# Loading the MLP weights during the convolution, and computing mish in groups of eight and six chunks instead of four

## The chip, the core and the metric

The kernel runs on one NeuronCore of a Trainium2 chip. The core has a matrix engine (TensorE, PE in the profile), a vector engine (VectorE, DVE), an engine for activation functions (ScalarE, ACT), a general engine (GpSimd, POOL) and a queue engine that starts transfers (SyncE, SP). Each runs its own list of instructions in order, and they wait for one another only through semaphores. Data lies in SBUF (128 partitions) and, for the results of matmuls, in PSUM. The metric is the time of one execution on the device in microseconds (us); "span" is the time from the first to the last instruction in the profiled execution.

## What is computed

One block of a network with 2048 tokens of 640 features. `A_ref` is a long convolution whose kernel is made from the parameters; `B_ref` is an MLP with the activation mish, h·tanh(log(1+exp(h))), and a hidden width of 1728.

```python
def _B_ref(x, w1, b1, w2):
    h = jnp.einsum("bsd,df->bsf", x, w1) + b1
    sp = jnp.log1p(jnp.exp(-jnp.abs(h))) + jnp.where(h > 0, h, jnp.zeros_like(h))
    act = h * jnp.tanh(sp)
    return jnp.einsum("bsf,fd->bsd", act, w2)

x = A_u
h = x + _A_ref(_layernorm(x, axis=-1), ...)      # convolution over the tokens, cut here
h2 = h + _B_ref(_layernorm(h, axis=-1), B_w1, B_b1, B_w2)
return h2
```

## The kernel before

The kernel is a sequence of stages. First come the tables and the convolution's kernel (parameters `AreT` ... `DskB`, scratch `rr`, `tth`, `Prr`, `Pii`, `Hr_t`, `Hin_t`, ...), then the forward transform and the products with the planes `PKc`, `PKs`, `qv` (results in `Yr_t`, `Ysn_t`), then the inverse transform, the residual sum in `xs`, the second layer norm and its transposition into `ln2T`, and last the MLP. SBUF is handed out by stacks of contexts: what is entered in `esA2` is given back when the kernel of the convolution is done, `esB` holds the transform's buffers, and `esC`, opened when `esB` and `esA` have been closed, holds everything of the MLP, its weights included. So the weights lie where buffers of the transform lay, and their load waits until these are no longer read:

```python
esC = ExitStack()
esC.__enter__()
EC = esC.enter_context
w1s = EC(nc.sbuf_tensor([P, ND, F], BF16))
w2s = EC(nc.sbuf_tensor([P, NFT, D], BF16))
b1s = EC(nc.sbuf_tensor([P, NFT], FP32))
mishT = EC(nc.sbuf_tensor([P, NFT, 2, 512], BF16))
NPD1 = 3
pd1 = EC(nc.psum_tensor([P, NPD1, FF], FP32))
po = EC(nc.psum_tensor([P, 2, 1024], FP32))
# ... (views of the weights in DRAM)
@block.gpsimd
def _(gp):
    gp.wait_ge(s_vyf.sem, h_done_v)          # the last residual sum
    gp.wait_ge(s_pei.sem, 2 * NFR)           # the last matmul of the inverse transform
    gp.wait_ge(s_ped.sem, 2 * NFR)
    gp.wait_ge(s_aed.sem, 4 * 2 * NFR)
    gp.dma_start(w1s[:], w1_v).then_inc(s_x.sem, 16)
    gp.dma_start(w2s[:, 0:13, :], w2_v).then_inc(s_x.sem, 16)
    # ... the last 64 rows of w2, and b1 in two pieces
w_loaded = s_x.n
```

The MLP works on four blocks of 512 tokens (`sc`). A block has 14 chunks of the hidden width (`ft`; 13 of 128 rows and one of 64). A chunk is five matmuls on PE (`dense1_chunk`, into one of three PSUM buffers), the addition of the bias by DVE into a slot of `ebuf` (`dve_h_evac`), then Exp, Ln(1+x) and Tanh on ACT, a chunk or a pair of chunks at a time, and the product h·tanh on DVE into `mishT` (`dve_mish_mult`). When all 14 products of a block are there, PE computes its four token tiles of the second product (`dense2_stile`, 28 matmuls each), and DVE adds them to `xs` (`dve_out_tile`). ACT works by groups of chunks; PE and DVE follow the same groups:

```python
NSLOT = 8
ebuf = EC(nc.sbuf_tensor([P, NSLOT, 3, FF], BF16))
GROUPS = [[0, 1, 2, 3], [4, 5, 6, 7], [8, 9, 10, 11], [12, 13]]

def dense1_chunk(pe, sc, ft):
    ci = sc * NFT + ft
    if ci >= NPD1:
        pe.wait_ge(s_vm.sem, ci - NPD1 + 1)      # PSUM buffer free: chunk ci-3 evacuated
    # ... five matmuls

def dense2_stile(pe, st):
    if st >= 2:
        pe.wait_ge(s_vo.sem, st - 1)             # PSUM buffer free: tile st-2 added
    sc = st // 4
    pe.wait_ge(s_vm2.sem, (sc + 1) * NFT)        # all 14 products of the block
    # ... 14 matmuls of 512 columns, 14 of 128

@block.tensor
def _(pe):
    pe.wait_ge(s_x.sem, w_loaded)
    for sc in range(SC):
        pe.wait_ge(s_aet.sem, min(NT, 4 * sc + 4))
        for gi, grp in enumerate(GROUPS):
            for ft in grp:
                dense1_chunk(pe, sc, ft)
            if sc >= 1:
                dense2_stile(pe, (sc - 1) * 4 + gi)
    for st in range(12, 16):
        dense2_stile(pe, st)

def act_group(ac, sc, grp):
    ac.wait_ge(s_vm.sem, base + grp[-1] + 1)     # the whole group is in ebuf
    # ... ops: pairs of chunks where two slots lie side by side, else single chunks
    for rows, h_ap, sp_ap, th_ap, n in ops:
        s_am.tick(ac.activation(sp_ap, h_ap, ACT.Exp))
    ac.wait_ge(s_am.sem, s_am.n)
    for rows, h_ap, sp_ap, th_ap, n in ops:
        s_am.tick(ac.activation(sp_ap, sp_ap, ACT.Ln, bias=cst[0:rows, 1:2]))
    ac.wait_ge(s_am.sem, s_am.n)
    for rows, h_ap, sp_ap, th_ap, n in ops:
        last = s_am.tick(ac.activation(th_ap, sp_ap, ACT.Tanh))

def dve_mish_mult(vc, sc, ft):
    vc.wait_ge(s_am.sem, act_done_val[(sc, ft)]) # the last Tanh of the chunk's group
    # ... h * tanh

@block.vector
def _(vc):
    for sc in range(SC):
        for gi, grp in enumerate(GROUPS):
            for ft in grp:
                dve_h_evac(vc, sc, ft)
            if gi >= 1:
                for ft2 in GROUPS[gi - 1]:
                    dve_mish_mult(vc, sc, ft2)
            if sc >= 1:
                dve_out_tile(vc, (sc - 1) * 4 + gi)
        for ft2 in GROUPS[-1]:
            dve_mish_mult(vc, sc, ft2)
    for st in range(12, 16):
        dve_out_tile(vc, st)
```

`dve_h_evac` of chunk number ci (counted over all blocks) also waits until the slot's previous owner, ci-NSLOT, has been multiplied.

Of the kernel before, what the change touches and what calls it, by code (L numbers as in the profile page):

```python
# [9 lines left out]
FP32 = mybir.dt.float32  # L10
BF16 = mybir.dt.bfloat16
# [19 lines left out]
def bass_sequential_preLN__ssm_conv_s4__dense_activation_mish__prompt_kernel(  # L31
# [4 lines left out]
    L = 2048  # L36
    D = 640
    F = 1728
    P = 128
    NT = L // P  # L40
    ND = D // P
    FF = 512
    HB = 256
    NFR = L // HB
    NB = 32
    NA = 8
    NFT = 14
    FLAST = F - 13 * P
# [9 lines left out]
    s_x = mkev("s_x")  # L58
    s_parT = mkev("s_parT")
    s_wk = mkev("s_wk")  # L60
# [8 lines left out]
    s_ak = mkev("s_ak")  # L69
    s_pe = mkev("s_pe")  # L70
    s_vev = mkev("s_vev")
    s_pef = mkev("s_pef")
    s_vpl = mkev("s_vpl")
    s_ped = mkev("s_ped")
    s_aed = mkev("s_aed")
    s_vyf = mkev("s_vyf")
    s_pei = mkev("s_pei")
# [14 lines left out]
    EP = esP.enter_context  # L92
# [10 lines left out]
    l2st = EP(nc.sbuf_tensor([P, NT, 2, 6], FP32))  # L103
    l2mv = EP(nc.sbuf_tensor([P, NT, 2], FP32))
    l2rs = EP(nc.sbuf_tensor([P, NT, 2], FP32))
    ln2T = EP(nc.sbuf_tensor([P, ND, L], BF16))
    ln2t = EP(nc.sbuf_tensor([P, 2, D], BF16))
    ident = EP(nc.sbuf_tensor([P, P], BF16))
    identf = EP(nc.sbuf_tensor([P, P], FP32))
# [2 lines left out]
    block = EP(nc.Block())  # L112

    x_tok = A_u.rearrange("b (t p) d -> p t (b d)", p=P)

    esA = ExitStack()
    esA.__enter__()
    EA = esA.enter_context
    PKc = EA(nc.sbuf_tensor([P, 2, D], BF16))
    PKs = EA(nc.sbuf_tensor([P, 2, D], BF16))  # L120
    qv = EA(nc.sbuf_tensor([P, D], BF16))
    AreT = EA(nc.sbuf_tensor([P, D], BF16))
    AimT = EA(nc.sbuf_tensor([P, D], BF16))
    BreT = EA(nc.sbuf_tensor([P, D], BF16))
    BimT = EA(nc.sbuf_tensor([P, D], BF16))
    CreT = EA(nc.sbuf_tensor([P, D], BF16))
    CimT = EA(nc.sbuf_tensor([P, D], BF16))
    ldtB = EA(nc.sbuf_tensor([P, D], BF16))
    DskB = EA(nc.sbuf_tensor([P, D], BF16))
    dtB = EA(nc.sbuf_tensor([P, D], FP32))  # L130
    rr = EA(nc.sbuf_tensor([P, D], FP32))
    tth = EA(nc.sbuf_tensor([P, D], FP32))
    Prr = EA(nc.sbuf_tensor([P, D], FP32))
    Pii = EA(nc.sbuf_tensor([P, D], FP32))
    lnst = EA(nc.sbuf_tensor([P, NT, 2, 6], FP32))
    lnmv = EA(nc.sbuf_tensor([P, NT, 2], FP32))
    lnrs = EA(nc.sbuf_tensor([P, NT, 2], FP32))

    esA2 = ExitStack()
    esA2.__enter__()  # L140
    EA2 = esA2.enter_context
    tmp4 = EA2(nc.sbuf_tensor([P, 4, HH], FP32))
    Hr_t = EA2(nc.sbuf_tensor([P, NB, HH], BF16))
    Hin_t = EA2(nc.sbuf_tensor([P, NB, HH], BF16))
# [12 lines left out]
    @block.gpsimd  # L157
    def _(gp):
        gp.dma_start(xs[:], x_tok).then_inc(s_x.sem, 16)
        s_x.n += 16  # L160
        s_pln.tick(gp.memset(mhalf[:], -0.5))
        s_pc.tick(gp.memset(identf[:], 0.0))
        gp.wait_ge(s_pc.sem, s_pc.n)
        s_pc.tick(gp.affine_select(out=identf[:], in_=identf[:], compare_op=ALU.not_equal, fill=1.0, base=0,
                                   pattern=[[-1, P]], channel_multiplier=1))
        s_pc.tick(gp.iota(qi[:, 0, 0:HB], [[1, HB]], base=0, channel_multiplier=0))
        s_pc.tick(gp.iota(qi[:, 0, HB:FF], [[1, HB]], base=0, channel_multiplier=0))
        gp.wait_ge(s_pc.sem, s_pc.n)
        s_pc.tick(gp.iota(qi[:, 0, HB:HB + 1], [[1, 1]], base=256, channel_multiplier=0))
        s_pc.tick(gp.iota(mci[:, 0:1], [[0, 1]], base=0, channel_multiplier=1))  # L170
        s_pc.tick(gp.iota(qi[:, 1, 0:HB], [[1, HB]], base=256, channel_multiplier=0))
# [117 lines left out]
    wk_loaded = s_wk.n  # L289
# [203 lines left out]
    kgen_done_vev = s_vev.n  # L493
    act_kgen_final = s_ak.n
# [62 lines left out]
    planes_done_vpl = s_vpl.n  # L557
# [13 lines left out]

    esA2.__exit__(None, None, None)

    esB = ExitStack()
    esB.__enter__()
    EB = esB.enter_context
# [193 lines left out]
    ln2T_done_a = s_aet.n  # L770

    esB.__exit__(None, None, None)
    esA.__exit__(None, None, None)

    if DEV_STAGE == "ln2T":
        @block.sync
# [8 lines left out]
    esC = ExitStack()  # L785
    esC.__enter__()
    EC = esC.enter_context
    w1s = EC(nc.sbuf_tensor([P, ND, F], BF16))
    w2s = EC(nc.sbuf_tensor([P, NFT, D], BF16))
    b1s = EC(nc.sbuf_tensor([P, NFT], FP32))  # L790
    mishT = EC(nc.sbuf_tensor([P, NFT, 2, 512], BF16))
    NPD1 = 3
    pd1 = EC(nc.psum_tensor([P, NPD1, FF], FP32))
    po = EC(nc.psum_tensor([P, 2, 1024], FP32))

    w1_v = B_w1.rearrange("(dt p) f -> p dt f", p=P)
    w2_v = B_w2[0:13 * P, :].rearrange("(ft p) d -> p ft d", p=P)
    w2_last = B_w2[13 * P:F, :]
    b1_v = B_b1[0:13 * P].rearrange("(ft p) -> p ft", p=P)
    b1_last = B_b1[13 * P:F]  # L800

    @block.gpsimd
    def _(gp):
        gp.wait_ge(s_vyf.sem, h_done_v)
        gp.wait_ge(s_pei.sem, 2 * NFR)
        gp.wait_ge(s_ped.sem, 2 * NFR)
        gp.wait_ge(s_aed.sem, 4 * 2 * NFR)
        gp.dma_start(w1s[:], w1_v).then_inc(s_x.sem, 16)
        gp.dma_start(w2s[:, 0:13, :], w2_v).then_inc(s_x.sem, 16)
        gp.dma_start(w2s[0:FLAST, 13, :], w2_last).then_inc(s_x.sem, 16)  # L810
        with nc.allow_non_contiguous_dma(reason="b1 small"):
            gp.dma_start(b1s[:, 0:13], b1_v).then_inc(s_x.sem, 16)
            gp.dma_start(b1s[0:FLAST, 13:14], b1_last.rearrange("(p o) -> p o", o=1)).then_inc(s_x.sem, 16)
        s_x.n += 5 * 16
    w_loaded = s_x.n

    SC = 4
    SW = L // SC
    NCH = SC * NFT
    out_tok = out.rearrange("b (t p) d -> p t (b d)", p=P)  # L820

    NSLOT = 8
    ebuf = EC(nc.sbuf_tensor([P, NSLOT, 3, FF], BF16))

    GROUPS = [[0, 1, 2, 3], [4, 5, 6, 7], [8, 9, 10, 11], [12, 13]]

    def slot_of(sc, ft):
        return (sc * NFT + ft) % NSLOT
# [14 lines left out]
    def dense2_stile(pe, st):  # L843
        cur = st % 2
        if st >= 2:
            pe.wait_ge(s_vo.sem, st - 1)
        sc = st // 4
        scb = sc % 2
        pe.wait_ge(s_vm2.sem, (sc + 1) * NFT)
        inst = None  # L850
        for ci2, (cs, ce) in enumerate(((0, 512), (512, 640))):
            for fi in range(NFT):
                rows = P if fi < NFT - 1 else FLAST
                inst = pe.matmul(po[:, cur, cs:ce] if cs == 0 else po[:, cur, 512:640],  # L854
                                 mishT[0:rows, fi, scb, (st % 4) * P:(st % 4 + 1) * P],
                                 w2s[0:rows, fi, cs:ce],
                                 start=(fi == 0), stop=(fi == NFT - 1))
        s_pe2.tick(inst)
# [7 lines that stand above are left out]
                for ft in grp:  # L866
                    dense1_chunk(pe, sc, ft)
                if sc >= 1:
                    dense2_stile(pe, (sc - 1) * 4 + gi)
        for st in range(12, 16):  # L870
            dense2_stile(pe, st)

# [41 lines left out]
    def dve_h_evac(vc, sc, ft):  # L914
        ci = sc * NFT + ft
        rows = P if ft < NFT - 1 else FLAST
        cur = ci % NPD1
        sl = slot_of(sc, ft)
        vc.wait_ge(s_pe1.sem, ci + 1)
        if ci - NSLOT >= 0:  # L920
            psc, pft = (ci - NSLOT) // NFT, (ci - NSLOT) % NFT
            vc.wait_ge(s_am.sem, act_done_val[(psc, pft)])
            vc.wait_ge(s_vm2.sem, ci - NSLOT + 1)
        s_vm.tick(vc.tensor_scalar(ebuf[0:rows, sl, 0, :], pd1[0:rows, cur, :], b1s[0:rows, ft:ft + 1], None,  # L924
                                    op0=ALU.add))

    def dve_mish_mult(vc, sc, ft):
        rows = P if ft < NFT - 1 else FLAST
        sl = slot_of(sc, ft)
        scb = sc % 2  # L930
        vc.wait_ge(s_am.sem, act_done_val[(sc, ft)])
        s_vm2.tick(vc.tensor_tensor(mishT[0:rows, ft, scb, :], ebuf[0:rows, sl, 0, :], ebuf[0:rows, sl, 2, :],  # L932
                                    op=ALU.mult))

    def dve_out_tile(vc, st):
        cur = st % 2
        vc.wait_ge(s_pe2.sem, st + 1)
        s_vo.tick(vc.tensor_tensor(xs[:, st, :], po[:, cur, 0:640], xs[:, st, :], op=ALU.add))  # L938
# [4 lines that stand above are left out]
            for gi, grp in enumerate(GROUPS):  # L943
                for ft in grp:
                    dve_h_evac(vc, sc, ft)
                if gi >= 1:
                    for ft2 in GROUPS[gi - 1]:
                        dve_mish_mult(vc, sc, ft2)
                if sc >= 1:
                    dve_out_tile(vc, (sc - 1) * 4 + gi)  # L950
            for ft2 in GROUPS[-1]:
                dve_mish_mult(vc, sc, ft2)
        for st in range(12, 16):
            dve_out_tile(vc, st)

# [6 lines left out]
        sy.wait_ge(s_out.sem, s_out.n)  # L962

    esC.__exit__(None, None, None)
    esP.__exit__(None, None, None)


# [26 lines left out]
```

## Time and profile before

| what | value |
|---|---|
| time, median of 5 runs | 550.38 us (549.83 to 551.48) |
| span of the profiled execution | 549.2 us |
| busy PE / DVE / ACT | 297.1 / 302.5 / 280.9 us |
| last residual sum before the MLP (xs, L726) starts | 353.40 us |
| weights' first DMA issued (L808) | 356.25 us |
| first matmul of the MLP (L838) | 372.41 us |
| first Exp of the MLP (L890) | 380.42 us |
| last token tile added (L938) starts | 546.17 us |

The stages stand one behind the other, so no engine is busy for much more than half of the span; what limits the time is read stage by stage, from the timeline in a stretch and from the idle time in front of each group of instructions. Lines named L838 and so on are lines of the kernel before.

### The profile page before, as it was taken

Reading aid. Unit: us, or ns where it says so; the run is one execution under the profiler, and the core shown is the slowest. Engines: PE = TensorE matmul, PEld = TensorE weight load, DVE = VectorE, ACT = ScalarE, POOL = GpSimd, SP = SyncE. Lnnn points to the kernel's source line nnn. Section 1 sums busy time; section 2 is a strip of 40 time slices with the busy share of each in tenths; the row PEclk is TensorE's granted clock in tenths of the full one; section 3 lists DMA queues with packets and bytes.
Section 4 is the critical chain, followed back from the end, with each engine's and each line's share of the span. In section 5 each row is a group of like instructions: output and inputs, shape, how many; then the busy total and the mean of one; then the engine's idle time right before and its main releaser. Section 6 shows DMA issues by size and latency. Waiting matters only on the chain.

```text
span 549.2 us, 6388 instructions
## 1 busy us (share of the span) xinstructions
PE 297.1 (54%) x2497; PEld 180.1 (33%) x2520; DVE 302.5 (55%) x657; ACT 280.9 (51%) x449; POOL 19.2 (4%) x35
## 2 busy tenths in 40 slices
PE   0000000996000069995777366518618979979967
PEld 0000000996000069932334134303203434434423
DVE  5897998000199830024999979804324544545511
ACT  1279938003960920000433316722996987969930
POOL 2002000000000000000000012220000000000000
PEclk9999999999999999999988979857877998989979
DMA  8300000000000000000000000091000000000001
GB/s 232 73 1 0 0 1 0 2 2 1 1 0 0 1 1 2 2 0 0 1 0 1 1 1 1 1 323 0 1 1 12 13 24 14 24 13 24 13 18 43
DMA packets 10126, 11.66 MB, mean 21 GB/s; under 512 B 6272, under 2 KB 8832, under 8 KB 10096
## 3 DMA queue, kind: packets, MB, share of 16 engines
q0 software_dynamic: 3088, 7.05, 4.5%
q1 hardware_dynamic: 7008, 4.20, 2.8%
q8 instruction: 20, 0.33, 0.2%
q14 instruction: 10, 0.08, 0.1%
HBM read 7.38 MB, written 2.62 MB: 18 GB/s over the span
## 4 chain that ended last, share of the span: by engine, by line
DVE 39%; ACT 26%; PE 24%; issue 6%; DMA 2%; POOL 2%; ACTq 0%; DVEq 0%; POOLq 0%
PE pk L476 7%; PE pk L478 7%; ACT ebuf L893 5%; ACT ebuf L890 5%; ACT ebuf L897 5%; PE po L854 4%; ACT L893 4%; ACT tmp L452 3%; PE pd L838 3%; DVE Hr_t L460 3%; PE pkf L520 3%; DMA b1s<-in_B_b_dram 2%; DVE xs L726 2%; ACT Hr_t L380 2%; DVE Hin_t L421 2%
## 5 line engine op out<-in xcount | busy, mean ns | idle before, releaser
L476 PE MATMUL pk<-Gb_t,Hr_t 128*32 128x8 bf16 x640 | 72.8, 200 | 160.1 <-DVE Hr_t L460 160.1
L476 PEld LDWEIGHTS pk<-Gb_t,Hr_t 128*32 128x32 bf16 x640 | 72.6, 150 | 160.2 <-DVE Hr_t L460 160.2
L838 PE MATMUL pd<-ln2T,w1s 128*128 128x512 bf16 (+1 forms) x270 | 69.1, 407 | 39.5 <-DVE ebuf L924 25.6
L854 PE MATMUL po<-w2s,mishT 128*128 128x512 bf16 (+1 forms) x444 | 73.5, 315 | 6.8 <-DVE mishT L932 6.2
L478 PE MATMUL pk<-Gb_t,Hin_t 128*32 128x8 bf16 x640 | 72.7, 200 | 0.0
L478 PEld LDWEIGHTS pk<-Gb_t,Hin_t 128*32 128x32 bf16 x640 | 72.6, 150 | 0.0
L924 DVE TENSOR_SCALAR ebuf<-pd,b1s 128x512 bf16<-128x512 f32 (+1 forms) x56 | 41.1, 746 | 36.0 <-PE pd L838 33.7
L635 ACT ACTIVATE Ub<-pd 128x512 bf16<-128x512 f32 x16 | 9.6, 597 | 94.0 <-PE pd L619 64.6
L838 PEld LDWEIGHTS pd<-ln2T,w1s 128*128 128x128 bf16 (+1 forms) x280 | 27.2, 103 | 75.4 <-DVE ebuf L924 28.1
L854 PEld LDWEIGHTS po<-w2s,mishT 128*128 128x128 bf16 x448 | 36.0, 101 | 48.1 <-issue 27.5
L452 ACT ACTIVATE tmp<-tth,cst 128x320 f32<-128x320 f32 x64 | 32.5, 555 | 29.9 <-DVE Hin_t L421 26.7
L619 PE MATMUL pd<-ln1pad,Wf 128*128 128x512 bf16 (+1 forms) x235 | 39.0, 326 | 15.9 <-ACT Ub L638 10.8
L890 ACT ACTIVATE ebuf<-ebuf 128x1024 bf16<-128x1024 bf16 (+2 forms) x32 | 28.5, 937 | 34.6 <-DVE ebuf L924 34.6
L489 DVE CAST Ktapb<-pk 32x512 bf16<-32x512 f32 x10 | 6.8, 679 | 67.7 <-PE pk L478 67.7
L932 DVE TENSOR_TENSOR mishT<-ebuf 128x512 bf16<-128x512 bf16 (+1 forms) x56 | 20.1, 419 | 40.0 <-ACT ebuf L897 40.0
L938 DVE TENSOR_TENSOR xs<-po,xs 128x640 bf16<-128x640 f32 x16 | 13.2, 823 | 41.1 <-PE po L854 41.1
L460 DVE TENSOR_TENSOR Hr_t<-Hr_t,tmp 128x320 bf16<-128x320 bf16 x64 | 30.3, 493 | 6.5 <-ACT tmp L452 6.5
L619 PEld LDWEIGHTS pd<-ln1pad,Wf 128*128 128x128 bf16 x240 | 20.6, 107 | 34.4 <-ACT Ub L638 12.3
L893 ACT ACTIVATE ebuf<-ebuf,cst 128x1024 bf16<-128x1024 bf16 (+2 forms) x32 | 31.6, 1034 | 0.2
L897 ACT ACTIVATE ebuf<-ebuf 128x1024 bf16<-128x1024 bf16 (+2 forms) x32 | 28.6, 941 | 0.2
L390 ACT ACTIVATE Hin_t<-tth 128x320 bf16<-128x320 f32 x64 | 23.2, 454 | 0.0
L380 ACT ACTIVATE Hr_t<-rr 128x320 bf16<-128x320 f32 x64 | 23.2, 453 | 0.0
(131 smaller groups left out, 425.3 us busy)
## 6 DMA issues: line engine op xcount, KB each, us to landing
xs<-in_A_u_dram POOLq DMA_DIRECT2D x1, 2560.0 KB, 12.1
out_dram<-xs SPq DMA_DIRECT2D x16, 160.0 KB, 1.8
w1s<-in_B_w_dram POOLq DMA_DIRECT2D x1, 2160.0 KB, 8.9
w2s<-in_B_w_dram POOLq DMA_DIRECT2D x1, 2080.0 KB, 13.9
WK<-Wf SPq DMA_DIRECT2D x8, 32.0 KB, 1.8
ldtB<-in_A_log_dt_dram SPq DMA_DIRECT2D x1, 160.0 KB, 3.2
DskB<-in_A_Dskip_dram SPq DMA_DIRECT2D x1, 160.0 KB, 3.3
w2s<-in_B_w_dram POOLq DMA_DIRECT2D x1, 80.0 KB, 13.4
```

Source lines behind the costliest of these rows:

```text
L380: s_ak.tick(ac.activation(Hr_t[:, b, :], rr[:, d0:d0 + HH], ACT.Exp, scale=float(b)))
L452: s_ak.tick(ac.activation(tb, tth[:, d0:d0 + HH], ACT.Sin, bias=cst[:, 2:3], scale=float(b)))
L460: s_vk.tick(vc.tensor_tensor(Hr_t[:, b, :], Hr_t[:, b, :], tb, op=ALU.mult))
L476: pe.matmul(pk[0:NB, cur, j * NA:(j + 1) * NA], Hr_t[:, :, dl], Gb_t[:, 0, :, dl], start=True, stop=False)
L478: inst = pe.matmul(pk[0:NB, cur, j * NA:(j + 1) * NA], Hin_t[:, :, dl], Gb_t[:, 1, :, dl], start=False, stop=True)
L619: inst = pe.matmul(o_ap, Wf[:, j, colbase:colbase + 128], ln1pad[:, 2 * f + j, cs:ce], start=(ji == 0), stop=(ji == len(jlist) - 1))
L838: inst = pe.matmul(pd1[0:rows, cur, :], w1s[:, dt, ft * P:ft * P + rows], ln2T[:, dt, sc * SW:(sc + 1) * SW], start=(dt == 0), stop=(dt == ...
L854: inst = pe.matmul(po[:, cur, cs:ce] if cs == 0 else po[:, cur, 512:640], mishT[0:rows, fi, scb, (st % 4) * P:(st % 4 + 1) * P], w2s[0:row ...
L890: s_am.tick(ac.activation(sp_ap, h_ap, ACT.Exp))
L893: s_am.tick(ac.activation(sp_ap, sp_ap, ACT.Ln, bias=cst[0:rows, 1:2]))
L897: last = s_am.tick(ac.activation(th_ap, sp_ap, ACT.Tanh))
L924: s_vm.tick(vc.tensor_scalar(ebuf[0:rows, sl, 0, :], pd1[0:rows, cur, :], b1s[0:rows, ft:ft + 1], None, op0=ALU.add))
```

## The change

The change has four parts.

1. The contexts are ordered anew. Parameters and scratch of the convolution's kernel move into `esA2`, which is given back early; a new `esW`, opened right there, holds the weights and `ln2T` until the end. `PKc`, `PKs`, `qv` and the first layer norm's statistics move into the outermost context.
2. The load of the weights is issued by GpSimd as soon as the convolution's kernel and its planes are done, ahead of the forward transform.
3. The groups become eight and six chunks, and `ebuf` gets 16 slots. PE computes two token tiles after each group.
4. The products of a block's last group are no longer made at the end of the block, but after the fifth chunk of the next block has been evacuated (`ft == 4`).

It is meant to take the wait for the weights off the path and to halve the number of changes between Exp, Ln and Tanh on ACT.

```diff
-    ln2T = EP(nc.sbuf_tensor([P, ND, L], BF16))
... (contexts: EA becomes EP for PKc, PKs, qv, lnst, lnmv, lnrs, and EA2 for AreT to Pii)
     esA2.__exit__(None, None, None)
 
+    esW = ExitStack()
+    esW.__enter__()
+    EW = esW.enter_context
+    w1s = EW(nc.sbuf_tensor([P, ND, F], BF16))
+    w2s = EW(nc.sbuf_tensor([P, NFT, D], BF16))
+    b1s = EW(nc.sbuf_tensor([P, NFT], FP32))
+    ln2T = EW(nc.sbuf_tensor([P, ND, L], BF16))
... (views of the weights, moved here)
+    @block.gpsimd
+    def _(gp):
+        gp.wait_ge(s_pef.sem, 4)
+        gp.wait_ge(s_vpl.sem, planes_done_vpl)
+        gp.wait_ge(s_vev.sem, kgen_done_vev)
+        gp.wait_ge(s_ak.sem, act_kgen_final)
+        gp.wait_ge(s_wk.sem, wk_loaded)
+        gp.dma_start(w1s[:], w1_v).then_inc(s_x.sem, 16)
+        gp.dma_start(w2s[:, 0:13, :], w2_v).then_inc(s_x.sem, 16)
... (the other three pieces as before; the old issue in front of the MLP is taken out)
-    NSLOT = 8
+    NSLOT = 16
-    GROUPS = [[0, 1, 2, 3], [4, 5, 6, 7], [8, 9, 10, 11], [12, 13]]
+    GROUPS = [[0, 1, 2, 3, 4, 5, 6, 7], [8, 9, 10, 11, 12, 13]]
... (PE)
                 if sc >= 1:
-                    dense2_stile(pe, (sc - 1) * 4 + gi)
+                    dense2_stile(pe, (sc - 1) * 4 + 2 * gi)
+                    dense2_stile(pe, (sc - 1) * 4 + 2 * gi + 1)
... (DVE)
                 for ft in grp:
                     dve_h_evac(vc, sc, ft)
+                    if sc >= 1 and ft == 4:
+                        for ft2 in GROUPS[-1]:
+                            dve_mish_mult(vc, sc - 1, ft2)
                 if gi >= 1:
                     for ft2 in GROUPS[gi - 1]:
                         dve_mish_mult(vc, sc, ft2)
                 if sc >= 1:
-                    dve_out_tile(vc, (sc - 1) * 4 + gi)
-            for ft2 in GROUPS[-1]:
-                dve_mish_mult(vc, sc, ft2)
+                    dve_out_tile(vc, (sc - 1) * 4 + 2 * gi)
+                    dve_out_tile(vc, (sc - 1) * 4 + 2 * gi + 1)
+        for ft2 in GROUPS[-1]:
+            dve_mish_mult(vc, SC - 1, ft2)
```

More of the change, by code (lines that the diff above doesn't have):

```diff
@@ L114, in bass_sequential_preLN__ssm_conv_s4__dense_activation_mish__prompt_kernel @@
     x_tok = A_u.rearrange("b (t p) d -> p t (b d)", p=P)
[L116 to L137, printed above, removed]
+    PKc = EP(nc.sbuf_tensor([P, 2, D], BF16))
+    PKs = EP(nc.sbuf_tensor([P, 2, D], BF16))
+    qv = EP(nc.sbuf_tensor([P, D], BF16))
+    lnst = EP(nc.sbuf_tensor([P, NT, 2, 6], FP32))
+    lnmv = EP(nc.sbuf_tensor([P, NT, 2], FP32))
+    lnrs = EP(nc.sbuf_tensor([P, NT, 2], FP32))
     esA2 = ExitStack()
@@ L141, in bass_sequential_preLN__ssm_conv_s4__dense_activation_mish__prompt_kernel @@
     EA2 = esA2.enter_context
+    AreT = EA2(nc.sbuf_tensor([P, D], BF16))
+    AimT = EA2(nc.sbuf_tensor([P, D], BF16))
+    BreT = EA2(nc.sbuf_tensor([P, D], BF16))
+    BimT = EA2(nc.sbuf_tensor([P, D], BF16))
+    CreT = EA2(nc.sbuf_tensor([P, D], BF16))
+    CimT = EA2(nc.sbuf_tensor([P, D], BF16))
+    ldtB = EA2(nc.sbuf_tensor([P, D], BF16))
+    DskB = EA2(nc.sbuf_tensor([P, D], BF16))
+    dtB = EA2(nc.sbuf_tensor([P, D], FP32))
+    rr = EA2(nc.sbuf_tensor([P, D], FP32))
+    tth = EA2(nc.sbuf_tensor([P, D], FP32))
+    Prr = EA2(nc.sbuf_tensor([P, D], FP32))
+    Pii = EA2(nc.sbuf_tensor([P, D], FP32))
     tmp4 = EA2(nc.sbuf_tensor([P, 4, HH], FP32))
@@ L572, in bass_sequential_preLN__ssm_conv_s4__dense_activation_mish__prompt_kernel @@
     esA2.__exit__(None, None, None)
+    esW = ExitStack()
[5 more added lines that the diff above has]
+    ln2T = EW(nc.sbuf_tensor([P, ND, L], BF16))
+    w1_v = B_w1.rearrange("(dt p) f -> p dt f", p=P)
+    w2_v = B_w2[0:13 * P, :].rearrange("(ft p) d -> p ft d", p=P)
+    w2_last = B_w2[13 * P:F, :]
+    b1_v = B_b1[0:13 * P].rearrange("(ft p) -> p ft", p=P)
+    b1_last = B_b1[13 * P:F]
+    @block.gpsimd
[7 more added lines that the diff above has]
+        gp.dma_start(w2s[:, 0:13, :], w2_v).then_inc(s_x.sem, 16)
+        gp.dma_start(w2s[0:FLAST, 13, :], w2_last).then_inc(s_x.sem, 16)
+        with nc.allow_non_contiguous_dma(reason="b1 small"):
+            gp.dma_start(b1s[:, 0:13], b1_v).then_inc(s_x.sem, 16)
+            gp.dma_start(b1s[0:FLAST, 13:14], b1_last.rearrange("(p o) -> p o", o=1)).then_inc(s_x.sem, 16)
+        s_x.n += 5 * 16
+    w_loaded = s_x.n
     esB = ExitStack()
@@ L772, in bass_sequential_preLN__ssm_conv_s4__dense_activation_mish__prompt_kernel @@
     esB.__exit__(None, None, None)
-    esA.__exit__(None, None, None)
     if DEV_STAGE == "ln2T":
@@ L787, in bass_sequential_preLN__ssm_conv_s4__dense_activation_mish__prompt_kernel @@
     EC = esC.enter_context
-    w1s = EC(nc.sbuf_tensor([P, ND, F], BF16))
-    w2s = EC(nc.sbuf_tensor([P, NFT, D], BF16))
-    b1s = EC(nc.sbuf_tensor([P, NFT], FP32))
     mishT = EC(nc.sbuf_tensor([P, NFT, 2, 512], BF16))
@@ L794, in bass_sequential_preLN__ssm_conv_s4__dense_activation_mish__prompt_kernel @@
     po = EC(nc.psum_tensor([P, 2, 1024], FP32))
[L796 to L815, printed above, removed]
     SC = 4
@@ L964, in bass_sequential_preLN__ssm_conv_s4__dense_activation_mish__prompt_kernel @@
     esC.__exit__(None, None, None)
+    esW.__exit__(None, None, None)
     esP.__exit__(None, None, None)
```

## The prediction
> **What bounds the kernel now.** I began with the page's busy times. They decide nothing: PE, DVE and ACT are each busy about half of the span. The two rows of slices show where the change can act: one slice, at 357 to 371 us, has no compute, and moves 323 GB/s.
>
> ```profile
> PE 297.1 (54%) x2497; PEld 180.1 (33%) x2520; DVE 302.5 (55%) x657; ACT 280.9 (51%) x449; POOL 19.2 (4%) x35
> ...
> GB/s 232 73 1 0 0 1 0 2 2 1 1 0 0 1 1 2 2 0 0 1 0 1 1 1 1 1 323 0 1 1 12 13 24 14 24 13 24 13 18 43
> ```
>
> Next, the timeline at this slice (start, duration, what, and in brackets the idle time before it and who ended it). PE does its last transposes of ln2T at 358.90 and then waits 12.82 us for the last piece of the weights, whose issue began at 356.25:
>
> ```profile
> 356.25 0.96 POOL L808 DMA_DIRECT2D w1s<-in_B_w_dram  x1
> ...
> 358.90 0.69 PE L681 MATMUL ptr<-ident,ln2t 128*128 128x128 bf16 x5 [0.88 <-ACT ln2T L765]
> ...
> 360.35 1.28 ACT L890 ACT_TABLE_LOAD   x1
> 372.41 5.30 PE L838 MATMUL pd<-ln2T,w1s 128*128 128x512 bf16 x12 [12.82 <-DMA b1s<-in_B_b_dram]
> ```
>
> Then the MLP, from the groups of instructions kept apart by shape, from 360 us on (busy us, mean ns). Ln needs a table load, and so does the Tanh after it: 16 groups, 32 loads of 1283 ns, 41 us. Exp after Tanh needs none.
>
> ```profile
> L893 ACT ACT_TABLE_LOAD x16 | 20.5, 1283 | 0.3
> L897 ACT ACT_TABLE_LOAD x16 | 20.5, 1283 | 0.3
> ```
>
> And last the busy time of the engines in stretches of the MLP (us: PE, PEld, DVE, ACT, POOL, then the granted clock). First two stretches from the first Exp of a block to its last Tanh:
>
> ```profile
> 417.50:450.90 33.40, 31.07 (x172) 14.44 (x173) 14.91 (x26) 32.25 (x32) 0.00 (x0) 0.98 0.06 20
> 455.10:488.50 33.40, 31.13 (x172) 14.44 (x173) 14.91 (x27) 32.25 (x32) 0.00 (x0) 0.98 0.06 20
> ```
>
> And stretches of 4 us, one of an idle PE and two of a busy one:
>
> ```profile
> 408.00:412.00 4.00, 0.00 (x0) 0.00 (x0) 0.12 (x1) 3.96 (x5) 0.00 (x0) 0.50 0.00 0
> ...
> 424.00:428.00 4.00, 4.00 (x20) 1.86 (x19) 3.13 (x6) 3.09 (x4) 0.00 (x0) 1.00 0.03 11
> 428.00:432.00 4.00, 3.95 (x28) 2.01 (x27) 1.61 (x4) 3.97 (x5) 0.00 (x0) 1.00 0.00 0
> ```
>
> ACT is busy 32.25 of 33.40 us: it is the bound. But PE stands right behind it. Between two blocks ACT waits as well: the first Exps of blocks 1, 2 and 3 start at 417.52, 455.09 and 492.66, so a block takes 37.57 us, about 4.2 of which ACT waits for the next block's first four evacuations.
>
> [...] the Exps end at 382.42, the load starts at 382.44 and the Ln at 383.74, so a change costs 1.30 us in all, and I use that. [...] the trace has two loads for each group, not three. [...] clock 0.50 at 408 to 412 where PE idles, matmuls of 512 columns every 0.43 us at 372.41 and every 0.22 later, and after an idle 3.48 us (452.41) it was slow again, while after one of about 2.2 us (396 to 400) the clock read 1.00.
>
> **The units**, all from the timeline of blocks 1 and 3. A warm chunk takes PE 1.08 us (evacuations start at 423.13, 424.21, 425.29). Four chunks and one tile take 8.54 (tiles are added at 421.94 and 430.48), so a tile takes 8.54 - 4.32 = 4.22. Starting cold costs about 2.3 more (the tile at 526.96 takes 6.51). An evacuation is 0.75, three together 2.05; four products are 1.43. ACT repeats a group of four in 8.70 (389.15 to 397.85): 2.00 + 1.30 + 2.19 + 1.30 + 2.00, less 0.09 overlap; the group of two takes 6.24.
>
> **Part 1 and 2, contexts and load.** No compute instruction goes or comes. PE can begin the MLP when its transposes end, 359.6; 372.41 - 359.65 = 12.8 us leave the path. The load (16.2 us from issue to landing, 356.25 to 372.4) now lies beside the forward transform at about 257, with some 85 us of slack.
>
> **Part 3, ACT.** The number of ACTIVATEs stays at 96; 16 of the 32 loads go, 20.5 us of ACT. A further pair of chunks adds 0.94 to Exp and Tanh and 1.04 to Ln. Group of eight: 3.89 + 1.30 + 4.27 + 1.30 + 3.89 = 14.65. Group of six (two pairs, one single, one of 64 rows): 3.05 + 1.30 + 3.42 + 1.30 + 3.05 = 12.1. A block needs 26.7 us of ACT, against 3 x 8.70 + 6.24 = 32.3 now. PE needs the same as ever, 14 x 1.08 + 4 x 4.22 = 32.0. So **PE becomes the bound**, and of the 5.6 us that ACT gains in a block little would be left, if a block did not now take 37.57.
>
> **Part 3 and 4, the path.** I follow it through.
> First block: PE starts at 359.65, cold; 12 matmuls at 0.43 and 28 at 0.215, and an evacuation, let the first Exp start at 371.95 (12.3 after PE's start, where it is 8.0 now: the larger group gives back 4.3). ACT ends the eight at 386.6 and the six at 398.6.
> Meanwhile PE has done three chunks ahead by 380.7 and waits, because DVE stands at the eight products until 386.6; then it starts cold, and has chunks 5 to 7 of block 1 ready at 398.3. DVE: six products from 398.65 to 400.9, three evacuations to 402.9, and there the second block's first Exp starts. ACT has waited 4.3 us, as much as now.
> Block 1: tiles 0 and 1 start at 400.9 after 2.6 us of idle PE. If PE is still warm, they end at 409.4, the six chunks at 415.9, tiles 2 and 3 at 424.4. ACT ends its eight at 417.5, its six at 429.6. From here PE has no gap: block 2 begins at 424.4, its fifth chunk is evacuated at 430.5, the six products of block 1 end at 432.7, before PE ends the eighth chunk at 433.0. Block 3 begins 32.0 later at 456.4, its tiles 8 and 9 end at 473.5, its last chunks at 480.0; the eight of ACT run from 466.8 to 481.4, the six to 493.5.
> End: today the span ends 549.2 - 526.06 = 23.1 after the last products begin, with four tiles behind them, the first cold. That tail stays: 493.6 + 23.1 = 516.7, or with a cold tile 0, 2.3 more: 519.0.
> In sum: 12.8 (weights) - 4.3 (first group), then 37.57 x 3 + 33.4 = 146.1 from the first Exp to the last Tanh before and 493.5 - 371.95 = 121.6 after, 24.5 less, or 22.2 if cold; together 31 to 33 us. Hand-offs between engines that I set at zero are some 0.1 us each, about 20 on the path, 2 us. I choose a span of 520, and with the 1.2 us by which the median lies above the span, 521.
>
> **Rivals.** (a) The long groups turn overlap into waiting. DVE executes in order, and products wait for the last Tanh of eight; if each block paid one such wait of 5 us on PE as block 1 does, plus a cold start of 2.3, blocks 2 and 3 would take 39 instead of 32: 521 + 14 = 535. Against it: from block 2 on PE's eighth chunk ends (433.0) after the products (432.7), though by 0.3 us. (b) Only the load is hidden, and the MLP stays at 37.57 a block: 550.4 - 12.8 + 4.3 - 5.6, the last for block 0, where PE has no tiles to do and ACT's gain must show: 536. For it: PE is busy 31.1 of 33.4 us already, so the table loads alone did not set the 37.57. Against it: the 37.57 has 4 to 5 us in which PE idles and then runs cold, which go. (c) The weights' traffic slows the transform: DVE paces it, and 16 us at a tenth slower would cost 1.6, so 523. (d) [...] Against it: the clock reads 1.00 in every 4 us in which PE is busy 4.00.
>
> **Range and chances.** The weights' 12.8 us are all but sure, and are 2.3% by themselves, less 4.3 for the first group. The rest hangs on PE running through blocks 2 and 3. Small slips put it at 517 to 527; rival (a) in one block gives 528; (b) and (d) are the tail above. Range 515 to 529. Faster by over 2% means below 539.4: 0.95. Within 2%: 0.04. Slower: 0.01.
>
> **What would show it.** Right: the weights' DMA near 257 us and the MLP's first matmul right behind the transposes, with no wait for a DMA; 16 table loads in place of 32 (20.5 us in all, and one for the first Exp); first Exp of the MLP 12.3 us after its first matmul; first Exps of blocks 2 and 3 about 32 us apart; clock 1.00 and PE busy nearly throughout from block 2 to tile 11; a tail of 23 us. Wrong: PE idling in blocks 2 and 3 with DVE's product as the releaser (a), blocks of 37 us (b), the transform's stretch of 257 to 353 longer (c), or warm matmuls slower than 0.22 us (d).

## The result, and the profile after

The changed kernel takes 520.54 us (median of 8 runs, 519.86 to 521.49) against 550.09 of the kernel before; the ratio is 0.9464, with a 95% interval of 0.9453 to 0.9475. The prediction was 521.0, with a range of 515 to 529. The lines of the MLP have new numbers: L839 is the first product (L838 before), L855 the second (L854), L892, L895 and L899 are Exp, Ln and Tanh (L890, L893, L897), L926 the evacuation (L924), L934 the product with tanh (L932).

The page's busy times and its row of transfers. PE and DVE have as many instructions as before. PE is busy 9.3 us less, at a mean granted clock of 0.962 (0.934 before), and ACT 22.5 us less. The burst of the weights has moved from slice 27 to slice 21:

```profile
PE 287.8 (56%) x2497; PEld 177.2 (34%) x2520; DVE 302.2 (58%) x657; ACT 258.4 (50%) x433; POOL 19.2 (4%) x35
...
GB/s 232 87 6 1 0 1 0 1 3 1 1 1 0 0 1 1 3 3 0 0 340 3 1 0 1 2 0 1 1 1 0 25 27 14 13 27 25 27 13 39
```

The timeline of GpSimd at the planes' end, and that of PE at the end of the transposes. The load is issued at 257.98, and PE's first matmuls of the MLP stand directly behind the transposes, with no wait for a DMA:

```profile
257.98 0.95 POOL L591 DMA_DIRECT2D w1s<-in_B_w_dram  x1 [209.46 <-DVE PKs L552]
```
```profile
358.82 0.69 PE L707 MATMUL ptr<-ident,ln2t 128*128 128x128 bf16 x5 [0.89 <-ACT ln2T L791]
359.31 20.56 PE L839 MATMUL pd<-ln2T,w1s 128*128 128x512 bf16 x83
```

The groups from 355 us on (busy us, mean ns): 16 table loads in place of 32.

```profile
L895 ACT ACT_TABLE_LOAD x8 | 10.3, 1283 | 0.1
L899 ACT ACT_TABLE_LOAD x8 | 10.3, 1283 | 0.1
```

The timeline of ACT: the four blocks' first Exps, with what ACT waited for in front of them. They lie 30.9, 33.7 and 32.2 us apart, where it was 37.1, 37.6 and 37.6 before:

```profile
370.75 3.90 ACT L892 ACTIVATE ebuf<-ebuf 128x1024 bf16<-128x1024 bf16 x4 [9.20 <-DVE ebuf L926]
...
401.66 3.89 ACT L892 ACTIVATE ebuf<-ebuf 128x1024 bf16<-128x1024 bf16 x4 [4.22 <-DVE ebuf L926]
...
435.35 3.90 ACT L892 ACTIVATE ebuf<-ebuf 128x1024 bf16<-128x1024 bf16 x4 [5.81 <-DVE ebuf L926]
...
467.57 3.90 ACT L892 ACTIVATE ebuf<-ebuf 128x1024 bf16<-128x1024 bf16 x4 [5.53 <-DVE ebuf L926]
```

And the busy time in these stretches (us: PE, PEld, DVE, ACT, POOL, then the clock). From block 1 on it is PE that has no gap: 33.32 of 33.69 us and 31.85 of 32.22. ACT, the bound before, has over 5 us to spare in each.

```profile
401.66:435.35 33.69, 33.32 (x182) 15.62 (x184) 18.20 (x32) 26.68 (x29) 0.00 (x0) 0.97 0.06 20
435.35:467.57 32.22, 31.85 (x181) 15.16 (x183) 18.30 (x32) 26.58 (x29) 0.00 (x0) 1.00 0.06 22
```

So the time came from two places: about 13 us in front of the MLP, and the MLP's own blocks. Which of the change's parts earned the second is not to be read off one trace; the experiments tell.

### The profile page after: what moved, and what is told of

The parts are those of the page before. It is cut to its first block, busy times and chain, and to the rows that moved or that the text cites. A ratio compares the mean times of both kernels' runs of the same rounds, so it can differ in the third digit from the quotient of the medians.

```text
span 518.0 us, 6360 instructions
## 1 busy us (share of the span) xinstructions
PE 287.8 (56%) x2497; PEld 177.2 (34%) x2520; DVE 302.2 (58%) x657; ACT 258.4 (50%) x433; POOL 19.2 (4%) x35
## 3 DMA queue, kind: packets, MB, share of 16 engines
HBM read 7.38 MB, written 2.62 MB: 19 GB/s over the span
## 4 chain that ended last, share of the span: by engine, by line
DVE 41%; PE 36%; ACT 17%; issue 4%; POOL 1%; ACTq 0%; DVEq 0%; POOLq 0%
PE po L855 10%; PE pd L839 7%; PE pk L472 7%; PE pk L474 7%; ACT tmp L448 4%; DVE Hr_t L456 3%; ACT ebuf L895 3%; PE pkf L516 3%; ACT ebuf L892 3%; DVE xs L752 2%; ACT Hr_t L376 2%; DVE Hin_t L417 2%; ACT ebuf L899 2%; DVE l2st L754 2%; DVE cttmp L678 2%
## 5 line engine op out<-in xcount | busy, mean ns | idle before, releaser
L855 PE MATMUL po<-w2s,mishT 128*128 128x128 bf16 (+3 forms) x440 | 70.1, 307 | 10.8 <-DVE mishT L934 9.9
L839 PE MATMUL pd<-ln2T,w1s 128*128 128x512 bf16 (+1 forms) x274 | 65.7, 398 | 9.6 <-DVE ebuf L926 9.1
L926 DVE TENSOR_SCALAR ebuf<-pd,b1s 128x512 bf16<-128x512 f32 (+1 forms) x56 | 41.2, 747 | 22.7 <-PE pd L839 22.3
L855 PEld LDWEIGHTS po<-w2s,mishT 128*128 128x128 bf16 x448 | 34.6, 99 | 48.0 <-issue 23.3
L448 ACT ACTIVATE tmp<-tth,cst 128x320 f32<-128x320 f32 x64 | 32.5, 555 | 29.8 <-DVE Hin_t L417 26.7
L645 PE MATMUL pd<-ln1pad,Wf 128*128 128x512 bf16 (+1 forms) x235 | 35.7, 305 | 19.1 <-ACT Ub L664 14.3
L839 PEld LDWEIGHTS pd<-ln2T,w1s 128*128 128x128 bf16 (+1 forms) x280 | 27.8, 103 | 45.2 <-DVE ebuf L926 11.3
L892 ACT ACTIVATE ebuf<-ebuf 128x1024 bf16<-128x1024 bf16 (+2 forms) x32 | 27.7, 936 | 25.8 <-DVE ebuf L926 25.8
L645 PEld LDWEIGHTS pd<-ln1pad,Wf 128*128 128x128 bf16 x240 | 19.1, 100 | 35.9 <-ACT Ub L664 16.1
L895 ACT ACTIVATE ebuf<-ebuf,cst 128x1024 bf16<-128x1024 bf16 (+2 forms) x32 | 30.7, 1030 | 0.1
L934 DVE TENSOR_TENSOR mishT<-ebuf 128x512 bf16<-128x512 bf16 (+1 forms) x56 | 19.4, 416 | 16.6 <-ACT ebuf L899 16.6
L899 ACT ACTIVATE ebuf<-ebuf 128x1024 bf16<-128x1024 bf16 (+2 forms) x32 | 27.7, 938 | 0.1
## 6 DMA issues: line engine op xcount, KB each, us to landing
xs<-in_A_u_dram POOLq DMA_DIRECT2D x1, 2560.0 KB, 12.5
```

Of the source, the lines that this page charges most:

```text
L448: s_ak.tick(ac.activation(tb, tth[:, d0:d0 + HH], ACT.Sin, bias=cst[:, 2:3], scale=float(b)))
L645: inst = pe.matmul(o_ap, Wf[:, j, colbase:colbase + 128], ln1pad[:, 2 * f + j, cs:ce], start=(ji == 0), stop=(ji == len(jlist) - 1))
L839: inst = pe.matmul(pd1[0:rows, cur, :], w1s[:, dt, ft * P:ft * P + rows], ln2T[:, dt, sc * SW:(sc + 1) * SW], start=(dt == 0), stop=(dt == ...
```

## The experiments

My theory: PE's 32 us of work a block is what is left as the bound, and what brings the block down to it is the order of work on DVE. The main rival: the gain in the blocks is that of the 16 table loads which were taken out of ACT. Each kernel is the changed one with the edit shown, unless it says otherwise. The kernel before, timed again beside each group of experiments, took 549.1 to 550.4 us, so a difference between kernels of different groups is good to about one microsecond.

### The load alone

The contexts and the early load, with the MLP's loops of the kernel before.

```diff
-    NSLOT = 16
-    GROUPS = [[0, 1, 2, 3, 4, 5, 6, 7], [8, 9, 10, 11, 12, 13]]
+    NSLOT = 8
+    GROUPS = [[0, 1, 2, 3], [4, 5, 6, 7], [8, 9, 10, 11], [12, 13]]
... (one token tile per group, the last group's products at the block's end)
```

> Only parts 1 and 2: contexts and early load, with the old 8 slots, groups of 4, 4, 4, 2 and the products at the block's end. Theory (the parts add up): 12.8 us less than before, about 537 us, first Exps of blocks 1 to 3 still 37.6 us apart. Rival (the load's traffic slows the transform and gives the gain back): 542 us or more, with the stretch from 253 to 353 us longer by several us.

Measured: 537.37 us, ratio to before 0.9769 (0.9744 to 0.9794): 12.5 us less. The first Exps stand at 365.96, 403.06, 440.40 and 477.84, 37.1 to 37.4 us apart. The transform did not pay for the traffic; here is the stretch that holds the load, before and then with the early load, with DVE's busy time, which sets its pace, as the third figure after the length:

```profile
253.00:318.00 65.00, 39.24 (x238) 20.61 (x240) 58.01 (x118) 22.81 (x64) 0.00 (x0) 0.91 0.00 1
```
```profile
253.00:318.00 65.00, 39.22 (x243) 19.94 (x241) 57.95 (x118) 22.81 (x64) 4.42 (x5) 0.92 0.28 69
```

The traffic is 69 GB/s in place of 1, and DVE does the same 118 instructions in the same time. The last residual sum starts at 353.47 us, where it was 353.40. The load's part is a plain 12.5 us.

### The load undone

```diff
     @block.gpsimd
     def _(gp):
-        gp.wait_ge(s_pef.sem, 4)
-        ... (the planes' semaphores)
+        gp.wait_ge(s_vyf.sem, h_done_v)
+        ... (the waits of the kernel before, and the block moved in front of the MLP)
```

> The changed kernel with the load issued where the kernel before issues it. Theory: 12.8 to 13.5 us more than the changed kernel, about 534 us; blocks as in the changed kernel. Rival (the wait for the weights gave cover to something else, so that the parts don't add up): less than 9 us more, under 530.

Measured: 533.08 us, ratio 0.9697 (0.9681 to 0.9713), 12.5 more than the changed kernel; PE again waits 12.9 us for the last piece of b1. The load is worth the same with either MLP, so the two halves of the change add up: 12.5 for the load and about 17 for the MLP.

### The products back at the block's end

```diff
                 for ft in grp:
                     dve_h_evac(vc, sc, ft)
-                    if sc >= 1 and ft == 4:
-                        for ft2 in GROUPS[-1]:
-                            dve_mish_mult(vc, sc - 1, ft2)
... (out tiles)
-        for ft2 in GROUPS[-1]:
-            dve_mish_mult(vc, SC - 1, ft2)
+            for ft2 in GROUPS[-1]:
+                dve_mish_mult(vc, sc, ft2)
```

> The changed kernel with the products of a block's last group back at the end of the block (part 4 undone). Theory (the order of DVE decides, since the next block's eight evacuations then wait for the last Tanh, and PE runs dry and cold behind them): first Exps of blocks 2 and 3 some 38 us apart in place of 32, in all 17 to 20 us more, about 539 us. Rival (ACT needs only 26.8 us of a block of 32, so the later evacuations are hidden in its slack): at most 3 us more, about 523.

Measured: 538.17 us, ratio 0.9788 (0.977 to 0.9807). That is 17.6 more than the changed kernel, and no better than the load alone: with its halved table loads and its 16 slots, but without the new place of the products, the MLP has gained nothing. The timeline of PE shows where it goes; each of the three lines is what PE does once the first evacuations of block 1, 2 and 3 set it free, with its wait in brackets:

```profile
401.21 7.75 PE L839 MATMUL pd<-ln2T,w1s 128*128 128x512 bf16 x25 [20.41 <-DVE ebuf L926]
...
439.86 7.21 PE L839 MATMUL pd<-ln2T,w1s 128*128 128x512 bf16 x25 [4.07 <-DVE ebuf L926]
...
477.96 6.93 PE L839 MATMUL pd<-ln2T,w1s 128*128 128x512 bf16 x25 [4.07 <-DVE ebuf L926]
```

DVE stands at a product until ACT's last Tanh of the block. Here is its timeline between blocks 0 and 1, first in this kernel and then in the changed one:

```profile
398.40 2.09 DVE L934 TENSOR_TENSOR mishT<-ebuf 128x512 bf16<-128x512 bf16 x6 [9.23 <-ACT ebuf L899]
400.42 2.05 DVE L926 TENSOR_SCALAR ebuf<-pd,b1s 128x512 bf16<-128x512 f32 x3
```
```profile
393.44 0.75 DVE L926 TENSOR_SCALAR ebuf<-pd,b1s 128x512 bf16<-128x512 f32 x1 [1.38 <-PE pd L839]
397.47 2.09 DVE L934 TENSOR_TENSOR mishT<-ebuf 128x512 bf16<-128x512 bf16 x6 [3.28 <-ACT ebuf L899]
```

Meanwhile the three PSUM buffers are full, so PE stands too, and 25 matmuls, 5.4 us at the 1.08 us that a chunk of five takes at full clock, take 6.9 to 7.8 after the wait. ACT in turn waits for the eight evacuations, 11.49, 10.96 and 10.68 us in front of blocks 1, 2 and 3. In the changed kernel five of these evacuations are done while ACT is still at work, the fifth at 393.44. PE takes two tiles behind each group in both kernels, so that part of the new order earns nothing by itself.

### ACT alone back in small groups

```diff
-            for grp in GROUPS:
+            for grp in [[0, 1, 2, 3], [4, 5, 6, 7], [8, 9, 10, 11], [12, 13]]:
                 for ft in grp:
                     ci = sc * NFT + ft
... (in ACT's loop only)
```

> The changed kernel with ACT alone back in groups of 4, 4, 4, 2: all 32 table loads are back, the order on PE and DVE and the 16 slots stay. Theory (PE's 32.0 us a block is the bound, and the order on DVE is what let it run): ACT needs 32.3 us a block without a stall, its first Exp comes 4.3 us earlier, the end within 3 us of the changed kernel, 518 to 524 us. Rival (the halved table loads are the gain): 16 loads of 1.28 us come back on the path, 538 to 542 us.

Measured: 520.59 us, ratio 0.9469 (0.9453 to 0.9484), against 520.54 for the changed kernel. All 32 table loads are back, and the time is the same. This is the run that decides: the rival is out. First ACT's waits for evacuations in the MLP of this kernel (us, times, longest), then the same line of the changed one:

```profile
ACT ebuf L892 <- DVE ebuf L926: 5.0, 1, 5.0
```
```profile
ACT ebuf L892 <- DVE ebuf L926: 25.8, 5, 9.2
```

With small groups ACT waits once, before its first Exp, and then works 129 us without a gap; with large ones it works less and waits in front of every block. PE's timeline in the kernel with small groups has the same pace, block 2 beginning at 425.58 and block 3 32.22 us later:

```profile
425.58 8.81 PE L839 MATMUL pd<-ln2T,w1s 128*128 128x512 bf16 x40
...
457.80 8.81 PE L839 MATMUL pd<-ln2T,w1s 128*128 128x512 bf16 x40
```

The first Exp comes 4.1 us earlier (366.64), since it waits for four evacuations and not for eight; the last Tanh comes 1.6 us later (495.82), but with two products behind it in place of six. The enlarged groups have bought back their own late start, and nothing more.

### Sixteen slots with the old order

The kernel of the load alone, with one more edit.

```diff
-    NSLOT = 8
+    NSLOT = 16
```

> The early load with 16 slots in place of 8, but the old groups and the old order of products and tiles. Theory (what holds a block at 37.4 us is the order on DVE: the products of the last group, and the last Tanh they wait for, stand in front of the next block's evacuations): still 37 us from first Exp to first Exp, 535 to 538 us. Rival (the eight slots held the evacuations back): blocks near 33 us and 525 us or less.

Measured: 536.26 us, ratio 0.9757 (0.9734 to 0.9781), blocks of 37.1 to 37.6 us. The 1.1 us to the load alone lie within the spread of the two (535.3 to 538.1, and 536.0 to 536.7), so the slots alone are not shown to bring anything. The kernel with small ACT groups has the same slots and the same 32 table loads and takes 15.7 us less; it differs from this one in the order on DVE and in that PE takes two tiles behind eight or six chunks. (The groups of eight and six can't run with eight slots: the evacuation of a block's ninth chunk would wait for the product of its first, which stands behind it in DVE's list. What was not tried is the kernel of the load alone, with its old groups and eight slots, and only the products of the last group moved. So it stays open whether the new place of the products is enough by itself.)

### Less work for PE

Four of the 14 terms of each token tile are left out, once in the changed kernel and once with ACT in the small groups, so the tiles' sums lack them.

```diff
-            for fi in range(NFT):
+            for fi in range(4, NFT):
... (the matmuls of a token tile; start at fi == 4)
```

> The changed kernel with four of the 14 terms of every token tile left out, so that PE needs 15.1 + 4 x 3.0 = 27.2 us a block in place of 32.2 (its output lacks these terms). Theory (PE is the bound, and the next one is ACT's 26.7 us and the 4.2 us for which it waits for products and three evacuations): blocks 2 and 3 fall to about 31 us, no further. Rival (PE was not the bound): they stay at 32.2.

> The same terms left out of the kernel with ACT in groups of 4, 4, 4 and 2. Theory: there ACT itself needs 32.3 us a block and has no gap, so its first Exps stay 32.3 us apart although PE has 5 us less to do; this is what 16 table loads cost once PE gives way, 1.3 us a block. Rival (PE is the bound there as well): blocks below 31 us.

Measured: 511.57 and 516.32 us. The first Exps of blocks 1 to 3, with the large groups and then with the small ones:

```profile
402.11 3.90 ACT L892 ACTIVATE ebuf<-ebuf 128x1024 bf16<-128x1024 bf16 x4 [4.22 <-DVE ebuf L926]
...
433.02 3.90 ACT L892 ACTIVATE ebuf<-ebuf 128x1024 bf16<-128x1024 bf16 x4 [4.22 <-DVE ebuf L926]
...
463.94 3.90 ACT L892 ACTIVATE ebuf<-ebuf 128x1024 bf16<-128x1024 bf16 x4 [4.22 <-DVE ebuf L926]
```
```profile
398.31 1.99 ACT L892 ACTIVATE ebuf<-ebuf 128x1024 bf16<-128x1024 bf16 x2
...
430.57 1.99 ACT L892 ACTIVATE ebuf<-ebuf 128x1024 bf16<-128x1024 bf16 x2
...
462.84 1.99 ACT L892 ACTIVATE ebuf<-ebuf 128x1024 bf16<-128x1024 bf16 x2
```

With large groups a block falls from 32.2 to 30.9 us and stops there, at 26.7 us of ACT and 4.2 us of waiting for six products and three evacuations. With small groups it stays at 32.3, where ACT has no gap. So PE was the bound of the changed kernel, but by 1.3 us a block only, and three limits lie close together: PE 32.2, ACT in small groups 32.3, ACT in large groups with its wait 30.9. The halved table loads begin to pay once PE has less to do.

### A small first group, a halved tail, and both

Theory now says where time is left: in front of the first Exp, where ACT waits for eight evacuations, and behind tile 11, where PE waits 7.1 us for the last products.

```diff
-            for grp in GROUPS:
+            for grp in ([[0, 1], [2, 3, 4, 5, 6, 7], [8, 9, 10, 11, 12, 13]] if sc == 0 else GROUPS):
```

> The changed kernel in which ACT takes the first block in groups of two, six and six (two table loads more). Theory (in the first block ACT is the bound and starts late because it waits for eight evacuations): first Exp 6 us earlier, last Tanh of the block 3 us earlier, and all of it reaches the end: 517 to 518 us. Rival (the first block is hidden, or PE's cold start eats it): within 1 us of the changed kernel.

```diff
-        for st in range(12, 16):
+        dense2_part(pe, 12, 0, 8)        # as dense2_stile, terms 0 to 7, waits for their products alone
+        dense2_part(pe, 13, 0, 8)
+        dense2_part(pe, 12, 8, NFT)
+        dense2_part(pe, 13, 8, NFT)
+        for st in range(14, 16):
             dense2_stile(pe, st)
```

> The changed kernel in which PE, behind tile 11, does the first eight of the 14 terms of tiles 12 and 13 before it waits for the last six products. Theory (PE idles 7.1 us in front of tile 12 and starts it cold): 4.8 us of matmuls move into that gap, and the idle left, 2.3 us, may or may not let the clock fall: 5 to 6.4 us less, 514 to 516 us. Rival (the tail is set by the last products alone, or accumulation in halves costs as much): within 1 us of the changed kernel.

> The small first group and the halved tail together. Theory (the two lie at the two ends of the MLP and PE is the bound between): the gains add up, 8 to 9 us, 511 to 513 us. Rival (one hides the other): no better than the better of the two, 514 to 516 us.

Measured: 517.75 us with the small first group (ratio 0.9423, 0.9403 to 0.9443), 513.28 with the halved tail (0.9349, 0.9327 to 0.9372), 511.08 with both (0.9299, 0.9279 to 0.9319): 2.8, 7.3 and 9.5 us less than the changed kernel. By the ratios to the kernel before, the differences are 2.3, 6.3 and 9.1. The gains add up to within 1 us. In the halved tail PE's wait in front of the last products is 2.67 us in place of 7.13, and the clock stays at 1.00 (492 to 500). From the end of tile 11 to the end of the span it takes 22.8 us in place of 28.6. The median of 513.28 is a little below the 514 that I gave as the lower end, and 0.6 us of it come from ahead of the tail, where the first tiles started at 399.05 and not at 399.62.

The small first group reached its number by another way than expected. Its first Exp came 6.0 us earlier (364.76), but the block's last Tanh only 1.9 (395.58 for 397.44) and not 3; its first eight chunks were evacuated 1.1 us later (ACT goes on at 371.83, where it begins at 370.75 in the changed kernel). The rest came from block 1: behind an idle 2.88 us PE's first two tiles took 8.51 us, as later tiles do at full clock, where they take 10.20 in the changed kernel, in part at a clock of 0.50. The first Exps of blocks 1 and 2 stand 32.00 us apart (399.80 and 431.80) for 33.69. The tail gave 1.0 us back. So a part of its 2.8 us is the clock's, and may differ in another execution: the mean granted clock of this kernel's four executions was 0.952 to 0.964.

### Whole blocks on PE

What is left in the MLP is PE's idle time between blocks 0 and 1. On top of both edits before:

```diff
-    NSLOT = 16
+    NSLOT = 28
-    ebuf = EC(nc.sbuf_tensor([P, NSLOT, 3, FF], BF16))
+    ebuf = EC(nc.sbuf_tensor([P, NSLOT, 2, FF], BF16))   # Tanh writes over Ln's result
... (PE)
+            for ft in range(NFT):
+                dense1_chunk(pe, sc, ft)
+            if sc >= 1:
+                for st in range((sc - 1) * 4, sc * 4):
+                    dense2_stile(pe, st)
... (DVE: all 14 evacuations of a block, with the products of the block before at ft == 4,
     in block 1 block 0's first eight at ft == 6 and its last six behind ft == 13;
     a block's first eight products between the second and third out tile)
```

> The small first group and the halved tail, and also: Tanh writes over Ln's result, so that the same 48 KB and 8 more hold 28 slots; PE computes a whole block of 14 chunks and then the four tiles of the block before; DVE evacuates all of block 1 before the products of block 0's last group. Theory (what is left over is PE's idle time of some 12 us between blocks 0 and 1): PE does 28 chunks in one go, idles about 5 us once, and ends 8.5 us earlier than without this, 502 to 504 us. Rival (the wait moves to ACT or to DVE's order in the later blocks): 508 us or more.

Measured: 505.68 us, ratio 0.9183 (0.9165 to 0.9201): 5.4 less than both edits before, and 14.9 less than the changed kernel; 1.7 us above the range that I gave. PE's timeline:

```profile
359.52 28.75 PE L839 MATMUL pd<-ln2T,w1s 128*128 128x512 bf16 x120
389.23 4.61 PE L839 MATMUL pd<-ln2T,w1s 128*128 128x512 bf16 x20 [0.95 <-DVE ebuf L945]
397.56 18.64 PE L855 MATMUL po<-w2s,mishT 128*128 128x512 bf16 x112 [3.72 <-DVE mishT L953]
416.14 8.81 PE L839 MATMUL pd<-ln2T,w1s 128*128 128x512 bf16 x40
425.21 6.77 PE L839 MATMUL pd<-ln2T,w1s 128*128 128x512 bf16 x30 [0.27 <-DVE ebuf L945]
...
448.80 8.81 PE L839 MATMUL pd<-ln2T,w1s 128*128 128x512 bf16 x40
```

PE runs through 28 chunks with one gap of 0.95 us, idles 3.7 us once, and from then on never more than 0.3 until the tail. Of the missing 3 us, 1.3 lie in two blocks of 32.66 us (416.14 to 448.80), where the prediction's sum has 32.0. Where the rest lies is open. The first four tiles, behind the idle 3.7 us, took 18.64 us, and the four of the next block 16.96; but in the kernel with both edits the first tiles lost as much (10.20 us for two). This is the fastest version that I have.

## Why the prediction was right, point by point

**The weights.** 12.8 us was the term; the first matmul came 13.1 us earlier, and the two runs on the load give 12.5 each. The fear that the traffic slows the transform (rival c) is refuted by DVE's 57.95 against 58.01 us. (The slice that the prediction calls free of compute has a tenth of PE and two tenths of ACT, the last transposes.)

**The first block.** First Exp 12.3 us after PE's start was the working: the 8.0 of before and 4.3 (the terms that it names add up to 11.9). It was 11.4 (359.31 to 370.75): the clock read 0.50 until 363, for 3.7 us, where the working had 12 cold matmuls of 0.43, 5.2 us. The groups of eight and six took ACT 14.6 and 12.1 us, as worked out.

**Blocks 1 to 3.** PE as the bound at 32.0 a block: 32.2 between blocks 2 and 3, and the last Tanh at 494.3 where the working had 493.5 warm and 2.3 later cold. The first tiles did lose clock, after PE had idled 2.77 us (0.50 to 0.54 from 400.5 to 404.0): 10.20 us for 8.50, so 1.7 and not 2.3. The margin of 0.3 us that keeps PE from waiting in block 2 is what the trace has: block 1's six products end at 433.25, and PE takes the first tile at 433.54. Rival (a), products that stop PE in every block, did not come about, but the run with the products back at the block's end shows that it was close by: their place alone decides over 17.6 us.

**The tail.** I kept it at 23.1; it was 23.7. Six products stand in it now and not two, 2.09 us for 0.75, which I forgot, and the cold tile was quicker, 5.74 for 6.51: its clock was back at 1.00 after about 3.0 us, where it took about 4.5 in the kernel before.

**The sum.** The working ended at 519.0 with cold tiles, and I chose 520, an estimate, for hand-offs (in the trace of before one from ACT to DVE took 0.03 us at 450.94, one from DVE to ACT 0.12 at 455.09, one from DVE to PE 0.15 at 526.96); the profiled span was 518.0. The 1.2 us between span and median were misread. They compare a profiled execution of 551.06 us with a median of 550.38, while each execution takes about 1.9 us more than its own span (551.06 and 549.2; 519.88 and 518.0). The changed kernel's profiled execution was 0.7 us faster than its median, so a span of about 518.7 is typical. The span was set 1.3 us too long and the step to the median 0.7 us too short; that 521.0 lies so close to 520.54 is in part luck. By medians the change is worth 29.6 us, by the two profiled spans 31.2. (The prediction takes 37.57 us for all three blocks of before; the first took 37.10. Its 520 comes from the path of times and does not depend on it.)

**What the prediction did not see.** It followed one path, part 3 and part 4 together, and so never asked which of the two pays. It counted 20.5 us of ACT as gone; they are gone, and are worth nothing at present, since the same order with 32 table loads ends at the same time. So the step from 32.3 to 26.7 us of ACT a block, by which the prediction makes PE the bound, is not what made the gain. What made it is the gap between the blocks, which the prediction sees (4.2 us of ACT's wait) but does not set apart from the table loads. In the kernel before, 4.2 to 4.7 us of ACT's idle time a block and PE's cold starts came from one place in DVE's list, where products that wait for the block's last Tanh stand in front of the evacuations that the next Exp waits for: between blocks 1 and 2 DVE's products start at 450.94 after a wait of 3.98 us for Tanh, PE resumes at 452.41 after 3.48 us, its clock reads 0.50 from 453 to 456, and ACT resumes at 455.09 after 4.18.

## What to carry to other kernels

DVE took its list in order here, and passed a late wait on to everything behind it: with the products at the block's end a wait of 9.23 us for Tanh held up evacuations whose matmuls were long done, and this order cost 17.6 us in all. Before taking work from the engine that looks like the bound, look at what ends its idle time, and move the instruction that waits for a later event behind those that others are waiting for. And when a change helps, undo its parts one at a time: here the part that did most to the busy times did nothing for the time.

## What the runs showed of the hardware that I had not expected

The clock of PE fell after an idle time between two of the kernel before, 2.31 us (to 400.13), which left it at 1.00, and 3.48 us (to 452.41), behind which it read 0.50; and it fell late. In the changed kernel PE idles from 396.86 to 399.62. These stretches of half a microsecond (PE's busy time first, the clock third from the end) show it still at full clock when PE resumes, at half clock from about 400.5, and back at full after some 3.5 us:

```profile
399.50:400.00 0.50, 0.38 (x2) 0.21 (x3) 0.50 (x2) 0.00 (x0) 0.00 (x0) 1.00 0.00 0
400.00:400.50 0.50, 0.45 (x4) 0.20 (x3) 0.50 (x2) 0.00 (x0) 0.00 (x0) 1.00 0.00 0
400.50:401.00 0.50, 0.50 (x3) 0.23 (x2) 0.50 (x2) 0.00 (x0) 0.00 (x0) 0.54 0.00 0
...
403.50:404.00 0.50, 0.50 (x3) 0.08 (x1) 0.00 (x0) 0.50 (x2) 0.00 (x0) 0.54 0.00 0
404.00:404.50 0.50, 0.50 (x3) 0.09 (x1) 0.00 (x0) 0.50 (x1) 0.00 (x0) 1.00 0.00 0
```

Gaps of nearly the same length went both ways. Here are the first two tiles in the changed kernel, with PE's idle time before them in brackets:

```profile
399.62 10.20 PE L855 MATMUL po<-w2s,mishT 128*128 128x512 bf16 x55 [2.77 <-DVE mishT L934]
```

With the load undone the gap in front of the same tiles is 2.62 us; they took 10.15, and the first Exps of blocks 1 and 2 stand 33.64 us apart (33.69 in the changed kernel). With the small first group the gap is 2.88 us; they took 8.51, as at full clock, and the Exps stand 32.00 apart. In the halved tail an idle 2.67 us left the clock at 1.00, while with four terms fewer a gap of 2.88 us (to 461.99) ended in 0.50, from 462 to 465. So between 2.6 and 2.9 us the length of the gap did not decide by itself, and a fall cost 1.7 us. What decides is not shown by these runs.
